# Token order scattered in step t = 9 of the GLU and the ids loaded in step t = 11, instead of t = 10 and t = 12

## The chip, the core and the metric

The kernel runs on one core of a Trainium2 chip. The metric is the device time of one execution in microseconds; smaller is better. One execution was also recorded by the hardware profiler, and every time inside the kernel that is named below is taken from that one recording, counted from the start of its span.

The engines are named as in the profile: PE (matmuls), DVE (the vector engine), ACT (the scalar engine), POOL (GpSimd) and SP (the engine that only issues transfers here).

## The reference

Three stages follow each other: attention with a sliding window and four sink positions, a routed layer with eight experts that gives every token to one expert, and a gated layer over all 1536 tokens.

```python
attn_out = softmax(mask(q @ k.T / 8)) @ v            # 2 x 8 heads x 768 x 64
x = attn_out, heads joined                           # 1536 x 512
e = argmax(x @ w_gate)                               # expert of each token, at most 384 tokens each
y[i] = gate[i] * relu(x[i] @ w1[e]) @ w2[e]          # 0 for a token beyond the 384
out = (sigmoid(y @ w_gate2) * (y @ w_val)) @ w_out   # d_ff = 1536, out is 1536 x 512
```

The last line is the gated layer, called the GLU below.

## The kernel before

**Order of the tokens.** The expert stage leaves the tokens sorted by expert, so row r of the GLU's input is some token of the original order. Which one, `order_ids` and `load_ids` establish: the tile `pi` (one DVE addition, line 701) says for each original token which sorted row it went to; twelve indirect transfers issued by POOL (line 703, one for 128 tokens, four bytes a token) scatter the token numbers into a table `idsd` in DRAM; one transfer issued by SP (line 709) reads the table back as the tile `ids`. The output rows are then written to DRAM with indirect transfers that take their row numbers from `ids`.

```python
def order_ids():
    nc.vector.tensor_tensor(out=pi, in0=pi_a, in1=pi_d, op=ALU.add)
    for i in range(NTILE):
        nc.gpsimd.indirect_dma_start(
            out=idsd_v[i], out_offset=bass.IndirectOffsetOnAxis(ap=pi[:, i:i + 1], axis=0),
...
def load_ids():
    nc.sync.dma_start(out=ids, in_=idsd.rearrange("(j p) o -> p (j o)", p=P))
```

The inputs of `pi`, `pi_a` and `pi_d`, are ready since the expert stage (function `order`, at 150 us).

**The GLU's steps.** The function `glu` works on three chunks of 512 tokens. Each chunk has 12 steps, one for each 128 of the 1536 hidden columns; t counts the steps of all chunks from 0, so t = 9 is the tenth step and t = 12 the first step of the second chunk. Step t does, in this order in the program:

- up to three halves of weight blocks are unpacked in the staging tiles (`conv_a`, lines 153 to 160, ACT and DVE);
- `up`: 24 matmuls (lines 171 to 173) into two banks `g`, then the sigmoid on ACT (line 1023), the product on DVE (1024), and its split into a high part `gh` (ACT, 1025) and a low part `gl` (DVE, 1027);
- at two fixed steps, `order_ids` and `load_ids`;
- the unpacked halves are split into `pair` (`conv_b`, lines 167 and 168), and SP is told to load the next weight block (line 145);
- `down` of the step before: 12 matmuls, three for each of the four banks `acc` (tokens m = 0 to 3 of 128 each);
- if t is the first step of a chunk, `finish` for the chunk that has just ended: for m = 0 to 3 a copy of the bank `acc` into a tile `o` (ACT for m = 0 and 2, line 1075; DVE for m = 1 and 3, line 1073), and `put_out`, the indirect write of that tile by POOL (line 1056).

The tiles `o` come from a pool of three (`cp`, bufs=3). The fourth copy of a chunk, m = 3 on DVE, reuses the tile of m = 0 and so waits until the write of m = 0 has landed. The next matmul into the bank of m = 3 waits for that copy.

**What sets the order.** Each engine runs its instructions in the order in which the program was written, and waits on semaphores for the others. The twelve scatters and the writes of the output stand on POOL's queue, the load of `ids` and the weight loads on SP's. A transfer from POOL signals on one of eight lanes in turn, so the ninth scatter waits until the first has landed.

Of the kernel before, what the change touches and what calls it, by code (L numbers as in the profile page):

```python
# [26 lines left out]
def kernel(  # L27
# [116 lines left out]
    def load_glu(g, q):  # L144
        nc.sync.dma_start(out=stage[q].bitcast(I32), in_=wd[g].bitcast(I32))

    def conv_a(parts, step):

        for q, n0, n1 in parts:
            raw = stage[q].bitcast(I32).rearrange("p (n t) -> p n t", t=2)  # L150
            l_, h_ = raw[:, n0:n1, 0], raw[:, n0:n1, 1]
            if step == 0:
                nc.scalar.activation(out=h_.bitcast(F32), in_=h_.bitcast(F32), func=AF.Copy, scale=2.0 ** -112)
                nc.vector.tensor_scalar(out=l_, in0=l_, scalar1=29, scalar2=None, op0=ALU.logical_shift_right)
            elif step == 1:
                nc.vector.scalar_tensor_tensor(
                    out=l_, in0=h_, scalar=3, in1=l_, op0=ALU.logical_shift_left, op1=ALU.bitwise_or
                )
            else:
                nc.vector.scalar_tensor_tensor(  # L160
                    out=l_, in0=h_, scalar=-2 ** 31, in1=l_, op0=ALU.bitwise_and, op1=ALU.bitwise_or
                )

    def conv_b(q, s, n0, n1, eng):
        f = stage[q].rearrange("p (n t) -> p n t", t=2)[:, n0:n1, 0]
        h_ = slot[s][:, 0, n0:n1]
        nc.scalar.copy(out=h_, in_=f)
        eng.tensor_sub(out=slot[s][:, 1, n0:n1], in0=f, in1=h_.bitcast(F32))
# [531 lines left out]
# [5 lines that stand above are left out]
                in_=ids0[:, i:i + 1], in_offset=None, bounds_check=N - 1, oob_is_err=False,  # L705
            )

    def load_ids():
        nc.sync.dma_start(out=ids, in_=idsd.rearrange("(j p) o -> p (j o)", p=P))
# [261 lines left out]
    def glu(yh, yl):  # L971
        with ExitStack() as st:
# [36 lines left out]
            def up(n, r, w):  # L1009
                ch = n // NPAIR  # L1010
                c = slice(r * P, (r + 1) * P)
                cols = slice(ch * 512, ch * 512 + w)
                pss = []
                for j in range(2):
                    wh, wl = block(n, j)
                    ps = ps_g.tile([P, 512], F32, tag=f"g{j}", name=f"g{j}")[:, :w]
                    for k in range(KD):
                        mm3(ps, wh[:, k, c], wl[:, k, c], yh[:, k, cols], yl[:, k, cols], k == 0, k == KD - 1)
                    pss.append(ps)
                gh = gp.tile([P, 512], F32R, tag="gh", name="gh", bufs=3)  # L1020
                gl = gp.tile([P, 512], F32R, tag="gl", name="gl", bufs=3)
                g = gp.tile([P, 512], F32, tag="g", name="g")[:, :w]
                nc.scalar.activation(out=g, in_=pss[0], func=AF.Sigmoid)  # L1023
                nc.vector.tensor_tensor(out=g, in0=g, in1=pss[1], op=ALU.mult)  # L1024
                nc.scalar.copy(out=gh[:, :w], in_=g)  # L1025
                k = last_rows(w)
                nc.vector.tensor_sub(out=gl[:, :w - k], in0=g[:, :w - k], in1=gh[:, :w - k].bitcast(F32))
                if k:
                    nc.vector.tensor_sub(
                        out=gh[:, w:w + k], in0=g[:, w - k:], in1=gh[:, w - k:w].bitcast(F32)  # L1030
                    )
                return gh, gl
# [5 lines left out]
            def down(t, m, gh, gl, w):  # L1038
                n, r = steps[t]
                wh, wl = block(n, 2)  # L1040
                first, last = t % NF == 0, t % NF == NF - 1
                c = slice(m * P, min(m * P + P, w))
                k = last_rows(w)
                if k and c.stop == w:
                    both = accs[m][:2 * k], gh[:, w - k:w + k], wh[:, r]
                    upper_ = accs[m][:k], gh[:, w - k:w], wl[:, r]
                    if first:
                        nc.tensor.matmul(*both, start=True, stop=False)
                    nc.tensor.matmul(*upper_, start=False, stop=False)
                    if not first:  # L1050
                        nc.tensor.matmul(*both, start=False, stop=last)
                else:
                    mm3(accs[m][:c.stop - c.start], gh[:, c], gl[:, c], wh[:, r], wl[:, r], first, last)

            def put_out(j, o):
                nc.gpsimd.indirect_dma_start(  # L1056
                    out=out_v[j], out_offset=bass.IndirectOffsetOnAxis(ap=ids[:, j:j + 1], axis=0),
                    in_=o, in_offset=None, bounds_check=N - 1, oob_is_err=False,
                )

            def finish(ch, m, w, both=False):
                n = min(P, w - m * P)
                o = zero if n < P else cp.tile([P, 512], F32, tag="o", name="o")
                k = last_rows(w)
                if k and n < P:
                    lo = cp.tile([P, 512], F32, tag="o", name="lo")
                    nc.scalar.copy(out=lo[:k], in_=accs[m][k:2 * k])
                    nc.vector.tensor_tensor(out=o[:k], in0=accs[m][:k], in1=lo[:k], op=ALU.add)
                elif both:
                    nc.scalar.copy(out=o[:n, :256], in_=accs[m][:n, :256])  # L1070
                    nc.vector.tensor_copy(out=o[:n, 256:], in_=accs[m][:n, 256:])
                elif m % 2:
                    nc.vector.tensor_copy(out=o[:n], in_=accs[m][:n])  # L1073
                else:
                    nc.scalar.copy(out=o[:n], in_=accs[m][:n])
                put_out(ch * 4 + m, o)
# [4 lines left out]
            def run(t0, t1, w, half, before):  # L1081

                ch = t0 // NF
                held = []

                for m in range((w + P - 1) // P, 4):
                    put_out(ch * 4 + m, zero)
                for t in range(t0, t1):
                    pend = []
                    n, r = steps[t]  # L1090
                    while half and len(pend) < 3:
                        x, h = half[0]
                        if todo[x][0] > n + 2:
                            break
                        half.pop(0)
                        pend.append((x, h))
                    parts = [(x % 4, h * 512, h * 512 + 512) for x, h in pend]
                    for step in range(3):
                        conv_a(parts, step)
                    g = up(n, r, w)  # L1100

                    if t == 10:
                        order_ids()
                    elif t == 12:
                        load_ids()
                    for x, h in pend:
                        conv_b(x % 4, todo[x][2], h * 512, h * 512 + 512, nc.vector)
                        if h and x + 4 < len(todo):
                            load_glu(todo[x + 4][1], x % 4)
                    if before and t < len(steps) - 2:  # L1110
                        full = w if t > t0 else 512
                        for m in range((full + P - 1) // P):
                            down(t - 1, m, *before, full)
                        if t % NF == 0:
                            for m in range(4):
                                finish(t // NF - 1, m, full)
                    held = (held + [g])[-3:]
                    before = g
                if t1 == len(steps):

                    ms = list(range((w + P - 1) // P))
                    if w % P:
                        ms = ms[-1:] + ms[:-1]
                    for m in ms:
                        down(t1 - 3, m, *held[0], w)
                    for m in ms:
                        down(t1 - 2, m, *held[1], w)
                        down(t1 - 1, m, *held[2], w)
                        finish(ch, m, w, m == ms[-1])
                return before  # L1130
# [117 lines left out]
```

## Time and profile before

| | |
|---|---|
| median of 3 runs | 625.35 us (622.54 to 626.94) |
| the profiled execution, its own time | 624.89 us |
| span of the profiled execution | 623.2 us |
| mean granted PE clock over the span | 0.986 of full |
| PE busy | 599.0 us, 96% of the span |
| DVE busy | 361.0 us, 58% |
| ACT busy | 302.4 us, 49% |
| POOL busy | 107.1 us, 17% |

The span lies 1.7 us under the time of its own execution, and that time 0.5 us under the median. In the rows below a line number L1073 is a line of the kernel, a square bracket in a timeline says how long the engine had been idle before and what ended that, and an x and a number is a count of instructions.

### The profile page before, as it was taken

Reading aid. Unit: us, or ns where it says so; the run is one execution under the profiler, and the core shown is the slowest. Engines: PE = TensorE matmul, PEld = TensorE weight load, DVE = VectorE, ACT = ScalarE, POOL = GpSimd, SP = SyncE. Lnnn points to the kernel's source line nnn. Section 1 sums busy time; section 2 is a strip of 40 time slices with the busy share of each in tenths; the row PEclk is TensorE's granted clock in tenths of the full one; section 3 lists DMA queues with packets and bytes.
Section 4 is the critical chain, followed back from the end, with each engine's and each line's share of the span. In section 5 each row is a group of like instructions: output and inputs, shape, how many; then the busy total and the mean of one; then the engine's idle time right before and its main releaser. Section 6 shows DMA issues by size and latency. Waiting matters only on the chain. (4 is left out here: it accounts for less than half of the span.)

```text
span 623.2 us, 9350 instructions
## 1 busy us (share of the span) xinstructions
PE 599.0 (96%) x3326; PEld 499.4 (80%) x3326; DVE 361.0 (58%) x879; ACT 302.4 (49%) x586; POOL 107.1 (17%) x161
## 2 busy tenths in 40 slices
PE   8999999999999999998999999999699999999995
PEld 4898988957877887886878888888588888999893
DVE  2556466545248838667779999931148811249811
ACT  3578677612268848667556555522025411225411
POOL 3159758360000000000000000034200000200002
PEclk9899999999999999999999999999799999999998
DMA  8989957124029919648335555540203420103001
GB/s 187 304 255 308 341 146 239 55 101 157 0 76 323 347 59 327 260 171 292 115 135 204 199 178 174 191 137 0 69 0 113 170 123 0 68 1 136 1 0 72
DMA packets 43630, 93.97 MB, mean 151 GB/s; under 512 B 5664, under 2 KB 24352, under 8 KB 39728
## 3 DMA queue, kind: packets, MB, share of 16 engines
q1 hardware_dynamic: 39872, 86.24, 41.9%
q0 software_dynamic: 2304, 6.09, 2.6%
q10 hardware_dynamic: 1392, 0.86, 0.5%
q8 instruction: 34, 0.56, 0.4%
q14 instruction: 28, 0.23, 0.1%
HBM read 82.63 MB, written 10.75 MB: 150 GB/s over the span
## 5 line engine op out<-in xcount | busy, mean ns | idle before, releaser
L172 PE MATMUL g<-yl,pair 128*128 128x512 f32 (+1 forms) x288 | 109.0, 379 | 0.3 <-DVE yl L806 0.3
L171 PE MATMUL g<-yh,pair 128*128 128x512 f32 (+1 forms) x288 | 109.1, 379 | 0.2 <-ACT yh L805 0.2
L173 PE MATMUL g<-yh,pair 128*128 128x512 f32 (+1 forms) x288 | 108.8, 378 | 0.0
L1025 ACT CAST gh<-g 128x512 fp32r<-128x512 f32 (+1 forms) x36 | 21.4, 594 | 119.3 <-DVE g L1024 115.3
L1024 DVE TENSOR_TENSOR g<-g,g 128x512 f32<-128x512 f32 (+1 forms) x36 | 23.4, 651 | 83.1 <-PE g L173 68.3
L136 DVE TENSOR_TENSOR pair<-stage,pair 128x1024 fp32r<-128x1024 f32 x54 | 64.5, 1221 | 10.0 <-ACT pair L135 9.8
L135 ACT CAST pair<-stage 128x1024 fp32r<-128x1024 f32 x64 | 65.7, 1051 | 0.8 <-PE u L773 0.8
L773 PE MATMUL u<-pair,hh 128*128 128x512 f32 x224 | 61.7, 401 | 2.8 <-ACT pair L135 1.5
L171 PEld LDWEIGHTS g<-yh,pair 128*128 128x128 f32 x288 | 54.5, 189 | 9.4 <-ACT yh L805 0.7
L172 PEld LDWEIGHTS g<-yl,pair 128*128 128x128 f32 x288 | 54.5, 189 | 8.7 <-issue 0.6
L173 PEld LDWEIGHTS g<-yh,pair 128*128 128x128 f32 x288 | 54.5, 189 | 7.8
L773 PE MATMUL u<-pair,xh 128*128 128x512 f32 x224 | 60.5, 397 | 0.1
L703 POOL DMA_INDIRECT idsd<-ids,pi x12 | 11.8, 983 | 276.5 <-DVE pi L701 273.1
L303 ACT ACTIVATE pt<-sc,neg 128x260 f32<-128x260 f32 (+1 forms) x96 | 44.6, 491 | 26.4 <-DVE neg L292 26.3
L171 PE MATMUL acc<-pair,gh 128*128 128x512 f32 x132 | 51.8, 393 | 5.5 <-DVE o L1073 5.5
L173 PE MATMUL acc<-pair,gl 128*128 128x512 f32 x132 | 51.7, 392 | 0.0
L172 PE MATMUL acc<-pair,gh 128*128 128x512 f32 x132 | 51.7, 392 | 0.0
L773 PEld LDWEIGHTS u<-pair,hh 128*128 128x128 f32 x224 | 40.5, 188 | 13.2 <-issue 4.4
L1023 ACT ACTIVATE g<-g 128x512 f32<-128x512 f32 (+1 forms) x36 | 20.5, 569 | 59.8 <-PE g L173 54.0
L773 PEld LDWEIGHTS u<-pair,xh 128*128 128x128 f32 x224 | 40.8, 188 | 10.2 <-ACT xh L747 1.7
L338 PE MATMUL pv<-v,pts 128*128 128x73 f32 x352 | 43.1, 275 | 0.0
L338 PEld LDWEIGHTS pv<-v,pts 128*128 128x128 f32 x352 | 42.3, 196 | 0.0
(163 smaller groups left out, 1020.3 us busy)
## 6 DMA issues: line engine op xcount, KB each, us to landing
stage<-in_we_dram SPq DMA_DIRECT2D x64, 512.0 KB
stage<-in_wd_dram SPq DMA_DIRECT2D x30, 1024.0 KB
vraw<-in_vr_dram SPq DMA_DIRECT2D x11, 288.0 KB
kraw<-in_kd_dram SPq DMA_DIRECT2D x22, 132.0 KB
qraw<-in_qd_dram SPq DMA_DIRECT2D x22, 128.0 KB
vt<-in_vt_dram SPq DMA_DIRECT2D x11, 256.0 KB
slots<-zero SPq DMA_DIRECT2D x1, 2048.0 KB
xs<-slots SPq DMA_DIRECT2D x8, 256.0 KB
```

What stands on the lines that cost most here:

```text
L135: nc.scalar.copy(out=t[:, 0], in_=raw)
L136: eng.tensor_sub(out=t[:, 1], in0=raw, in1=t[:, 0].bitcast(F32))
L171: nc.tensor.matmul(ps, ah, bh, start=start, stop=False)
L172: nc.tensor.matmul(ps, ah, bl, start=False, stop=False)
L173: nc.tensor.matmul(ps, al, bh, start=False, stop=stop)
L303: nc.scalar.activation(out=pt_[i][:, h, :w], in_=scs_[n][j][:, :w], func=AF.Exp, scale=-1.0, bias=neg_[i][:, h:h + 1],)
L338: nc.tensor.matmul(pv_[n][:, h], pts_[n, h // 2][:, h % 2, j], vb[kb][:, 4 * a + h], start=(h == 0 and j == 0), stop=(h == 3 and j == len( ...
L703: nc.gpsimd.indirect_dma_start(out=idsd_v[i], out_offset=bass.IndirectOffsetOnAxis(ap=pi[:, i:i + 1], axis=0), in_=ids0[:, i:i + 1], in_of ...
L773: nc.tensor.matmul(ps, a, b, start=start, stop=stop)
L1023: nc.scalar.activation(out=g, in_=pss[0], func=AF.Sigmoid)
L1024: nc.vector.tensor_tensor(out=g, in0=g, in1=pss[1], op=ALU.mult)
L1025: nc.scalar.copy(out=gh[:, :w], in_=g)
```

## The change

Two constants change. `order_ids` is called in step t = 9 and not 10, `load_ids` in step 11 and not 12; each stands at the same place within its step.

```diff
                     g = up(n, r, w)
 
-                    if t == 10:
+                    if t == 9:
                         order_ids()
-                    elif t == 12:
+                    elif t == 11:
                         load_ids()
                     for x, h in pend:
                         conv_b(x % 4, todo[x][2], h * 512, h * 512 + 512, nc.vector)
```

On DVE, the place is between the `up` of step 9 and the `up` of step 10. In the names below `g_` and a number is a bank of an `up`, and L168 is the last split of a weight half before the pause in the weight work.

```order
 L1027 TENSOR_TENSOR gl<-g,gh 128x512
+L701 TENSOR_TENSOR pi<-pi_a,pi_d 128x12
 L168 TENSOR_TENSOR pair_91<-stage_84,pair_91 128x512
-L1024 TENSOR_TENSOR g<-g,g_5869 128x512
-L1027 TENSOR_TENSOR gl<-g,gh 128x512
-L701 TENSOR_TENSOR pi<-pi_a,pi_d 128x12
+L1024 TENSOR_TENSOR g<-g,g_5906 128x512
+L1027 TENSOR_TENSOR gl<-g,gh 128x512
```

The addition `pi` moves up over one product, one `gl` and one split; the bank numbers change with the numbering alone.

On SP, the rows around the load of `ids`, with the semaphores that each waits for, are these before:

```order
244 L145 DMA stage_83<-in_wd_dram 128x2048 [waits DMAHW2_49,DVE_49]
245 L145 DMA stage_84<-in_wd_dram 128x2048 [waits DMAHW3_49,DVE_49]
246 L709 DMA ids<-idsd 128x12x1 [waits DMASW4_49,DMASW5_49,DMASW3_49,DMASW6_49,DMASW2_49,DMASW7_49,DMASW1_49,DMASW0_49]
247 L145 DMA stage_85<-in_wd_dram 128x2048 [waits DMAHW4_49,DVE_49]
248 L145 DMA stage_86<-in_wd_dram 128x2048 [waits DMAHW5_49,DVE_49]
```

In the changed kernel these rows are the same, as is all of SP's queue and all of POOL's: no weight load stands between the old place and the new one. The load of `ids` waits for all eight lanes of POOL's transfers (DMASW0 to DMASW7).

## Rows read from the trace of the kernel before

**Rows 1.** The page, part 1: busy time, share of the span and instructions.

```profile
PE 599.0 (96%) x3326; PEld 499.4 (80%) x3326; DVE 361.0 (58%) x879; ACT 302.4 (49%) x586; POOL 107.1 (17%) x161
```

**Rows 2.** The page, part 2: granted PE clock in 40 slices of 15.6 us.

```profile
PEclk9899999999999999999999999999799999999998
```

**Rows 3.** Waits, 430 to 450 us: in total, times, longest.

```profile
DVE o L1073 <- DMA out_dram<-o,ids: 8.9, 1, 8.9
...
PE acc L171 <- DVE o L1073: 5.5, 1, 5.5
```

**Rows 4.** Timeline of PE, 429 to 444 us: start, duration, engine, line.

```profile
430.43 0.39 PE L171 MATMUL g<-yh,pair 128*128 128x512 f32 x1
...
437.69 0.39 PE L173 MATMUL acc<-pair,gl 128*128 128x512 f32 x1
443.52 0.80 PE L171 MATMUL acc<-pair,gh 128*128 128x512 f32 x1 [5.45 <-DVE o L1073]
```

**Rows 5.** Timeline of DVE, 380 to 480 us.

```profile
408.23 0.69 DVE L1027 TENSOR_TENSOR gl<-g,gh 128x512 fp32r<-128x512 f32 x1 [0.69 <-ACT gh L1025]
408.84 0.69 DVE L168 TENSOR_TENSOR pair<-stage,pair 128x512 fp32r<-128x512 f32 x1
411.66 0.69 DVE L1024 TENSOR_TENSOR g<-g,g 128x512 f32<-128x512 f32 x1 [2.13 <-PE g L173]
...
413.65 0.17 DVE L701 TENSOR_TENSOR pi<-pi_a,pi_d 128x12 int32<-128x12 f32 x1
419.82 0.69 DVE L1024 TENSOR_TENSOR g<-g,g 128x512 f32<-128x512 f32 x1 [6.01 <-PE g L173]
...
442.78 0.69 DVE L1073 COPY o<-acc 128x512 f32<-128x512 f32 x1 [8.87 <-DMA out_dram<-o,ids]
```

**Rows 6.** Timeline of POOL, 360 to 623 us.

```profile
414.09 1.02 POOL L703 DMA_INDIRECT idsd<-ids,pi  x1 [273.14 <-DVE pi L701]
...
419.27 0.98 POOL L703 DMA_INDIRECT idsd<-ids,pi  x1 [0.30 <-issue]
...
428.26 0.98 POOL L703 DMA_INDIRECT idsd<-ids,pi  x1 [0.30 <-issue]
439.92 0.98 POOL L1056 DMA_INDIRECT out_dram<-o,ids  x1 [10.68 <-issue]
...
534.84 0.98 POOL L1056 DMA_INDIRECT out_dram<-o,ids  x1 [90.08 <-ACT o L1075]
```

**Rows 7.** Line 709: duration in ns, first and last start in us.

```profile
L709 SPq EVENT_SEMAPHORE  x4: 17/28/28, 432.3 to 435.9; - x4
L709 SPq DMA_DIRECT2D ids<-idsd x1: 377/377/377, 436.0 to 436.0; - x1
```

**Rows 8.** Windows: length, busy time of each engine (count), PE clock, DMA share, GB/s.

```profile
281.40:283.20 1.80, 0.51 (x3) 0.26 (x3) 1.80 (x2) 1.50 (x2) 0.00 (x0) 1.00 0.97 303
...
413.00:415.00 2.00, 2.00 (x10) 1.67 (x9) 0.77 (x2) 0.01 (x1) 0.91 (x1) 1.00 0.30 119
...
441.00:443.00 2.00, 0.00 (x0) 0.00 (x0) 0.22 (x1) 0.00 (x0) 1.49 (x2) 0.60 0.48 184
...
443.52:448.32 4.80, 4.80 (x11) 3.84 (x12) 1.24 (x2) 0.62 (x1) 0.98 (x1) 0.51 0.29 109
...
449.00:451.00 2.00, 2.00 (x10) 1.63 (x9) 0.00 (x0) 0.60 (x1) 0.00 (x0) 1.00 0.03 8
```

**Rows 9.** Timeline of DVE, 525 to 545 us: the next chunk's end.

```profile
539.12 0.69 DVE L1073 COPY o<-acc 128x512 f32<-128x512 f32 x1 [3.75 <-DMA out_dram<-o,ids]
```

**Rows 10.** Waits of PE, 450 to 623 us.

```profile
PE acc L1051 <- DVE gh L1029: 0.3, 1, 0.3
```

**Rows 11.** SP: its timeline, 405 to 445 us.

```profile
409.56 0.33 SPq L145 DMA_DIRECT2D stage<-in_wd_dram  x1
435.95 0.38 SPq L709 DMA_DIRECT2D ids<-idsd  x1
```

**Rows 12.** Waits of SP's queue over the span.

```profile
SPq L145 <- DVE pair L168: 209.1, 18, 65.5
```

**Rows 13.** Line 477, the scatters of the attention stage: min, median and max in ns.

```profile
L477 POOL DMA_INDIRECT slots<-xg,si x12: 977/1083/1223, 38.3 to 131.7; - x12
```

## The prediction

> **What bounds the kernel now.** The page's first part is read first: PE is busy 96% of the span [rows 1], so only work taken off PE, or a hole in PE's row, can move the time much. The second part shows where a hole could be: the granted PE clock is full from the third slice on, with one digit 7 in slice 29, about 436 to 452 us [rows 2]. The waits of that stretch name it: PE waits 5.5 us for the DVE copy L1073, and that copy waits 8.9 us for the first output write to land [rows 3]. This is the first step of the GLU's second chunk, t = 12: the fourth copy of the finished chunk needs the tile of the first, whose write cannot start before `ids` is there.
>
> How much stands in that hole? At full clock 33 matmuls start between 430.43 and 437.69 us, 32 steps in 7.26 us or 0.227 us each, so the next was due at 437.92; it started at 443.52 [rows 4]. That is 5.60 us. Then the clock: it is at 0.60 on average between 441 and 443, so it fell to the lower level (1.2 of 2.4 GHz) in there, after PE had stood still for about 3.3 us, and from 443.52 to 448.32 it was 0.51 while 11 matmuls took 4.80 us; by 449 it was full again [rows 8]. Eleven at 0.227 take 2.50 us, so the slow matmuls lost 2.30. The whole hole is worth 7.90 us, and no change of this chain can give more.
>
> **The chain that ends in the hole.** Link by link: `pi` on DVE starts at 413.65 [rows 5]; the first scatter at 414.09, the twelfth at 428.26, one every 1.29 us, POOL having sat idle 273 us until `pi` [rows 6]; SP's last wait for a scatter ends at 435.9, 7.6 us after the twelfth was issued [rows 7]; the load of `ids` is issued at 435.95 [rows 11]; the first output write follows at 439.92 [rows 6]; the fourth copy starts at 442.78 [rows 5]; PE at 443.52 [rows 4]. From `pi` to the copy that is 29.13 us, and nothing in it but `pi` waits for a step of the GLU. So what counts is how far `pi` moves, not how far `load_ids` does.
>
> **The change part by part.** *`order_ids` one step up.* A step of the GLU at full clock is 36 matmuls, 36 x 0.227 = 8.2 us, but `pi` doesn't move by that. On DVE step 9 was late, behind weight unpacking: its last instruction, L1027, starts at 408.23, and L168 behind it at 408.84 [rows 5]. The new `pi` takes L168's place at 408.84 in place of 413.65: 4.81 us earlier. Its inputs are long there and POOL is idle, so the twelve scatters move by the same 4.81, from 414.09 to 409.28 and from 428.26 to 423.45.
>
> *`load_ids` one step up.* It stands behind the same weight load and ahead of the same one on SP's queue, and POOL's queue is unchanged too. SP comes to it after the load at 409.56 [rows 11] and then waits for the scatters, so the earlier place itself is worth nothing; it only follows the scatters, 435.95 - 4.81 = 431.14. What is queued behind it on SP, the next weight loads, waits for DVE's L168 of later steps, 209.1 us in all over 18 waits [rows 12], so it doesn't come free later than before.
>
> *The rest follows.* Output write at 439.92 - 4.81 = 435.11, fourth copy at 437.97, PE at 438.71, where it was due at 437.92: 0.79 us of the hole is left. Does the clock still fall? A stop of PE of 1.3 us in the window 281.40 to 283.20 left it at 1.00 [rows 8], and the fall in the hole came after some 3.3 us; so no, and the 2.30 us go too. The sum is 4.81 + 2.30 = 7.11 us.
>
> *Costs.* `pi` now stands ahead of L168, which starts 0.17 us later; the DVE instruction behind it idled 2.13 us for PE [rows 5], so this is covered. Were that cover gone, it would cost those 0.17 us. No instruction and no transfer is added.
>
> *What is late next.* After 450 us PE waits 0.3 us in all [rows 10], and the weight loads follow DVE, which follows PE; so all that comes after should slide up by the whole 7.1 us. The end of the next chunk shows the same chain with `ids` already there: its write starts at 534.84 [rows 6], its fourth copy waits 3.75 us until 539.12 [rows 9], and PE doesn't wait at all.
>
> *Bounds of the forecast.* The link that varies is the write's landing: 2.86 us from issue to copy in the first chunk (439.92 to 442.78) but 4.28 in the second (534.84 to 539.12). I take 2.86, since the quiet stretch is the same one; with 4.28, 1.42 us less is gained, 5.7. At the other end the hole closes wholly, 7.9.
>
> *Two rules weighed against it.* The scatters now start while the weight load issued at 409.56 is moving; in the old place they started in the window 413 to 415, where the DMA engines were at 0.30 and after which nothing was loaded [rows 8]. The first scatters may therefore land late, and the ninth waits for the first. Bound: if not one of them moved before 414.09, the chain would be where it is now, and the gain nothing; in between I take half of 4.81. The Trainium skill's page "DMA: Bandwidth & Descriptors", section "Issuing engines are not separate DMA queues", speaks for that: transfers from POOL and from SP run on the same engines and interleave, whoever started them. It is the first rival below.
>
> The other: more DVE work now stands beside the scatters, one L168, one L1024 and one L1027, 0.69 us each. If each held POOL up for its whole length, the chain would lose 2.07 us. Against it speaks the scatter at 419.27, which ran beside the L1024 at 419.82 and took 0.98 us like the others [rows 5, 6]; for it, that in the attention stage, with DVE far busier, a scatter took up to 1.223 us against a least of 0.977 [rows 13]. The Trainium skill's page "SBUF — State Buffer", section "SBUF: two separate sides", has such a rule: a DVE instruction in a mode that uses both ports locks GpSimd out while it writes descriptors. The rows here show no such lock at 419 us.
>
> **The rivals.**
> - *Scatters late beside the weight load.* Gain 2.4 us by the chain instead of 4.81; the hole left is 3.2 us, just short of where the clock fell, so I count the 2.3 us of the clock as half kept: 625.35 - 2.4 - 1.15 = 621.8. For: the overlap is real. Against: a scatter of 128 x 4 bytes is tiny, and only four of the twelve are waited for by others.
> - *DVE holds POOL up.* Gain 4.81 - 2.07 + 2.30 = 5.0, so 620.3. Against: the row at 419.27.
> - *The clock falls all the same.* Gain 4.81 alone: 620.5. Against: the clock stayed up through the other stops after 20 us.
> - *The change doesn't do what it says.* `load_ids` has the same neighbours on SP, so if the scatters did not start from `pi` alone, nothing would move: 625.4. Against: POOL's 273 us of idle ended by `pi` [rows 6].
> - *Slower, by the lane.* Scatter nine, now due at 419.60 us, waits until scatter one has landed. The old ninth was due at 424.4 and went out on time. If the weight load held the first scatter back beyond 424.4, 15 us after its issue, every further microsecond would push the whole chain and PE with it; landing 18 us after its issue it would give about 628. Nothing in the rows is that late: the twelfth took 7.6 us.
>
> **How the numbers follow.** The profiled execution: span 623.2 - 7.1 = 616.1, its own time 624.89 - 7.1 = 617.8. The median of the runs lies 0.46 above that execution, so the forecast is 625.35 - 7.1 = 618.2. Chances: the forecast with its bounds (617.4 to 619.7) 0.68; scatters late 0.14; the clock falls all the same 0.06; nothing moves 0.05; DVE holds POOL up 0.04; slower 0.03. The runs of before spread from 622.54 to 626.94, 0.4% to either side, so a measurement tells about 1%, here 6.3 us, from no change. The forecast lies just beyond that line and its own bounds on both sides of it: I count 0.56 of its 0.68 as faster by over 1%, and the rest, with most rivals, as within 1%; a little of the rivals that keep the clock goes to faster. Of the slower rival only the far end, a landing over 21 us after the issue, would pass 1%. That gives 0.57, 0.41 and 0.02. The range runs from 616.4, the hole closed and a fast draw of the runs, to 621.7, which takes in the clock and the DVE rivals and half of the late scatters.
>
> **What would show it.** In the changed profile: `pi` at 408.8, first scatter near 409.3, one every 1.29 us, last one near 423.5; load of `ids` near 431.1; first output write near 435.1; fourth copy near 438.0; PE's wait for it under 1 us, up to 2.2; no digit under 9 in the clock of slice 29; the rest of the GLU 7 us earlier, with PE still not waiting. Wrong it would be if the scatters' landing stretched (load of `ids` later than 433), if the wait moved to another tile, or if the clock fell somewhere else.

## The result, and the profile after

The changed kernel takes 619.37 us (median of 16 runs, 616.48 to 621.67) against 624.63 (16 runs, 620.84 to 628.61), so the medians are 5.3 us apart. The ratio worked out from all these runs is 0.9904, with a 95% interval from 0.9885 to 0.9924, or 6.0 us less (4.7 to 7.2). The forecast was 7.1 us less and 618.2 us, with a range of 616.4 to 621.7. The profiled execution has a span of 617.9 us.

The runs of one kernel spread by up to 0.6% either way, and the profile shows part of why. This is the granted clock of the changed kernel in 40 slices, to be read beside [rows 2]:

```profile
PEclk9999999999999999997999999999999999999998
```

The 7 of slice 29 is gone, but a 7 stands in slice 19, in the expert stage, where the kernel before had none. That stage isn't touched by the change, and the two spans differ for this reason too. So the change is read in the stage that it touches: from the first matmul of line 172, where the GLU begins, to the issue of the last output write. Before, that is 327.18 to 617.43 us, 290.25 us; after, 327.90 to 612.54, 284.64 us. The GLU is 5.61 us shorter, and this is the number to explain.

The waits of the changed kernel, 400 to 450 us, answer to [rows 3]:

```profile
DVE o L1073 <- DMA out_dram<-o,ids: 8.8, 1, 8.8
...
PE acc L171 <- DVE o L1073: 2.1, 1, 2.1
```

PE still waits for the fourth copy, but 2.1 us in place of 5.5. Its timeline, as in [rows 4]:

```profile
438.37 0.39 PE L173 MATMUL acc<-pair,gl 128*128 128x512 f32 x1
440.85 0.50 PE L171 MATMUL acc<-pair,gh 128*128 128x512 f32 x1 [2.09 <-DVE o L1073]
```

The next matmul was due at 438.37 + 0.23 = 438.60, so the hole is 2.25 us in place of 5.60. The clock stayed at 1.00 in every window of 2 us from 436 to 460, so the 2.30 us of slow matmuls are gone. These are the two windows around the hole, as in [rows 8]:

```profile
438.00:440.00 2.00, 0.76 (x4) 0.30 (x2) 0.00 (x0) 0.00 (x0) 1.39 (x3) 1.00 0.34 131
440.00:442.00 2.00, 1.15 (x5) 0.97 (x6) 1.28 (x2) 0.57 (x1) 1.70 (x2) 1.00 0.67 256
```

Both together are 5.65 us (5.60 - 2.25 + 2.30), against the 5.61 measured. DVE, POOL and the load of `ids` on SP, as in [rows 5, 6, 11]:

```profile
408.90 0.69 DVE L1027 TENSOR_TENSOR gl<-g,gh 128x512 fp32r<-128x512 f32 x1 [0.69 <-ACT gh L1025]
409.51 0.16 DVE L701 TENSOR_TENSOR pi<-pi_a,pi_d 128x12 int32<-128x12 f32 x1
409.60 0.68 DVE L168 TENSOR_TENSOR pair<-stage,pair 128x512 fp32r<-128x512 f32 x1
...
440.11 0.69 DVE L1073 COPY o<-acc 128x512 f32<-128x512 f32 x1 [8.77 <-DMA out_dram<-o,ids]
```

```profile
409.95 1.22 POOL L703 DMA_INDIRECT idsd<-ids,pi  x1 [272.23 <-DVE pi L701]
411.48 0.98 POOL L703 DMA_INDIRECT idsd<-ids,pi  x1 [0.30 <-issue]
412.76 0.98 POOL L703 DMA_INDIRECT idsd<-ids,pi  x1 [0.30 <-issue]
414.04 1.22 POOL L703 DMA_INDIRECT idsd<-ids,pi  x1 [0.30 <-issue]
...
421.48 0.97 POOL L703 DMA_INDIRECT idsd<-ids,pi  x1 [1.09 <-issue]
...
425.33 0.98 POOL L703 DMA_INDIRECT idsd<-ids,pi  x1 [0.30 <-issue]
437.26 0.98 POOL L1056 DMA_INDIRECT out_dram<-o,ids  x1 [10.95 <-issue]
```

```profile
433.21 0.38 SPq L709 DMA_DIRECT2D ids<-idsd  x1
```

All of this execution lies 0.67 us later by step 9 (L1027 at 408.90 against 408.23), and in that frame `pi` moved by exactly the 4.81 us forecast. But from `pi` to the fourth copy it is now 440.11 - 409.51 = 30.60 us, not 29.13. Of the 1.47 more, 1.21 lie between the first and the twelfth scatter (15.38 us against 14.17): two scatters took 1.22 us, the first and the fourth, where they had taken 1.02 and 0.98, and the ninth began 1.09 us after the end of the eighth and not 0.30, which is 0.79 more. The other 0.26 lie behind the twelfth scatter. For the ninth's delay the profile names nothing that POOL waited for (`<-issue`).

### The profile page after: what moved, and what is told of

The parts are those of the page before. It is cut to its first block, busy times and chain, and to the rows that moved or that the text cites. A ratio compares the mean times of both kernels' runs of the same rounds, so it can differ in the third digit from the quotient of the medians.

```text
span 617.9 us, 9350 instructions
## 1 busy us (share of the span) xinstructions
PE 596.4 (97%) x3326; PEld 496.9 (80%) x3326; DVE 361.6 (59%) x879; ACT 302.5 (49%) x586; POOL 107.4 (17%) x161
## 5 line engine op out<-in xcount | busy, mean ns | idle before, releaser
L1024 DVE TENSOR_TENSOR g<-g,g 128x512 f32<-128x512 f32 (+1 forms) x36 | 23.4, 649 | 77.6 <-PE g L173 66.0
```

## The experiments

No run takes one of the two constants alone. By the order of the queues it would show nothing new: with `order_ids` in 9 and `load_ids` left in 12 every queue holds the same instructions in the same order as the changed kernel, and with 10 and 11 the same as the kernel before. That the move of `load_ids` is worth nothing is argued from this order, as in the prediction.

The table puts all runs side by side. GLU is the stretch defined above, and hole is the time that PE stood still behind the fourth copy. (The copy belongs to step 12; the matmul that waits for it is in the `down` of step 13.) Chain is `pi` to the fourth copy. The clock column says whether the granted clock fell in the hole or within 2 us behind it. The stretches are read from one recorded execution of each kernel; the ratio is to runs of the kernel before that were taken along with it, with its 95% interval.

| run | GLU, us | hole, us | clock | chain, us | ratio to before |
|---|---|---|---|---|---|
| before | 290.25 | 5.60 | fell | 29.13 | 1 |
| changed | 284.64 | 2.25 | full | 30.60 | 0.9904 (0.9885 to 0.9924) |
| e1, scatter in t = 8 | 286.42 | 2.44 | fell | 36.38 | 0.9944 (0.9918 to 0.9970) |
| e2, before, tile of its own | 282.28 | 0 | full | | 0.9883 (0.9849 to 0.9916) |
| e3, before, PE kept busy | 288.89 | 1.70 idle | full | 30.04 | 0.9949 (0.9925 to 0.9973) |
| e4, load behind the ids | 286.05 | 3.63 | full | 31.95 | 0.9956 (0.9923 to 0.9989) |
| e5, scatter in t = 11 | 298.78 | 14.28 | fell | 29.65 | 1.0147 (1.0089 to 1.0205) |
| e6, load in t = 13 | 284.47 | 2.05 | full | 30.39 | 0.9880 (0.9839 to 0.9921) |
| e7, scatter in t = 4 | 295.83 | 0 | fell earlier | | 1.0042 (1.0008 to 1.0077) |
| e8, changed, tile of its own | 282.27 | 0 | full | | 0.9831 (0.9789 to 0.9872) |
| e9, pi behind the split | 286.21 | 2.16 | fell | 29.89 | one execution |
| e10, changed again | 284.79 | 2.34 | full | 30.67 | one execution |

**e2: the fourth copy gets a tile of its own.** The places of before are kept.

```diff
                 o = zero if n < P else cp.tile([P, 512], F32, tag="o", name="o")
+                if ch == 0 and m == 3:
+                    o = gp.tile([P, 512], F32, tag="gl", name="o4", bufs=3)
```

> The kernel before with its old places, but the fourth copy of the first chunk goes to a tile of its own (a free buffer of the gl tiles), so that it needn't wait for the first output write. Theory (the tile reuse is what ties PE to the ids): the copy runs at once, hole 0 though the ids come as late as before, clock full, gain 7.9 us, ratio 0.987. Rival (PE would meet the late ids elsewhere, at a later tile or bank): a new wait of several us within the next steps, ratio 0.995 or above.

The two copies on DVE in its timeline (m = 1 and 3; the line is 1075 in this kernel, which has two lines more), and the only wait of PE from 430 us on:

```profile
438.82 1.28 DVE L1075 COPY o<-acc 128x512 f32<-128x512 f32 x2
```

```profile
PE acc L1051 <- DVE gh L1029: 0.3, 1, 0.3
```

Both copies run back to back, and PE doesn't wait for the fourth copy, although the first output write is issued as late as 445.93. The GLU is 7.97 us shorter than before, against 7.90 forecast for the whole hole; the ratio 0.9883 agrees with 0.987. No new wait takes the hole's place. This shows the reuse of the tile to be what ties PE to the ids, and prices the hole with its clock.

**e8: the same tile in the changed kernel.**

> The changed kernel and the tile of its own for the fourth copy together. Theory (the change acts through the fourth copy's wait alone): hole 0, and the same time as with that tile and the old places, ratio 0.987 to 0.989. Rival (the change is worth something besides, or costs something, by the scatters beside the last weight load): a ratio off that by over 0.3%.

The GLU takes 282.27 us against 282.28 in e2: with the wait for the tile gone, the change is worth nothing in the GLU, and costs nothing. The ratio of 0.9831 lies off e2's 0.9883 by more than the 0.3% that the rival named, but the two intervals overlap, and the traces show no difference in the GLU. These two are the fastest versions, at medians of 615.31 and 616.69 us.

**e5: the scatter one step later.** From the kernel before:

```diff
-                    if t == 10:
+                    if t == 11:
                         order_ids()
```

> The kernel before with the scatter one step later (order_ids in t = 11, load_ids left in t = 12). Theory (in the stretch without weight loads the chain from pi to the fourth copy has a fixed length near 29 us, so each us of pi is a us of the hole): pi 8.2 us later, hole 13.7 us in place of 5.6, chain 28.5 to 30 us, clock lost about as before; ratio 1.013. Rival (something else than pi holds the ids, and pi's place counts only in part): hole under 10 us, ratio under 1.008.

```profile
423.21 0.16 DVE L701 TENSOR_TENSOR pi<-pi_a,pi_d 128x12 int32<-128x12 f32 x1
...
452.86 0.69 DVE L1073 COPY o<-acc 128x512 f32<-128x512 f32 x1 [20.80 <-DMA out_dram<-o,ids]
```

Counted from the start of the GLU, `pi` is 8.16 us later than before, and the chain is 29.65 us, 0.52 longer. The hole grows by the sum of both, 8.68 us, and the GLU by 8.53. So in the stretch without weight loads each microsecond of `pi` is a microsecond of the hole.

**e3: PE kept busy with matmuls of no use.** From the kernel before:

```diff
+                            if t == NF and m == 3:
+                                idle = ps_g.tile([P, 512], F32, tag="g0", name="idle")
+                                for _ in range(22):
+                                    nc.tensor.matmul(idle, ones, ones.unsqueeze(1).to_broadcast([P, 4, P]), start=True, stop=True)
                             down(t - 1, m, *before, full)
```

> The kernel before with 22 extra matmuls of no use in the hole at t = 12, just ahead of the matmuls that wait for the fourth copy. Theory (of the 7.9 us, 2.3 are the clock that falls while PE stands still): the granted clock stays at 1.00 through 441 to 448, the wait for the copy ends where it did, gain 2.3 us, ratio 0.996. Rival (the fall costs nothing, since the matmuls after it have slack, or it comes all the same): ratio 1.000.

The edit doesn't put the matmuls quite where the expectation has them. They run ahead of the last three matmuls of the finished chunk, a step before the hole, and so make all of PE's later work 5 us late instead of filling the hole itself:

```profile
433.14 4.92 PE L1116 MATMUL idle<-ones 128*128 128x512 bf16 x22
...
447.82 0.50 PE L171 MATMUL acc<-pair,gh 128*128 128x512 f32 x1 [1.55 <-DVE o L1073]
```

For the question it comes to the same: PE stands still for 1.70 us and not for the 5.60 of before, and the clock is 1.00 in all windows from 438 to 450. The GLU is 1.36 us shorter, in an execution whose chain was 0.91 longer (30.04 against 29.13), and 2.30 - 0.91 = 1.39. So the clock's 2.30 us of the hole are shown apart from the idle time; the ratio's interval holds the 0.996.

**e1: the scatter one more step up.** From the changed kernel:

```diff
-                    if t == 9:
+                    if t == 8:
                         order_ids()
```

> The scatter one more step up (order_ids in t = 8, load_ids in t = 11). Theory (the hole in PE at t = 12 goes with the place of pi on DVE, link by link): pi starts 5.6 us earlier than in the changed kernel, so even with a chain 1.5 to 4 us longer than the 29.1 us of before the fourth copy is ready before PE wants the bank; hole 0, clock full, gain about 7.9 us, ratio to before 0.987. Rival (the scatters lose to the weight loads that they now run beside what they gain by the earlier start): the ninth scatter waits several us for the first, the hole stays at 2 us or more, ratio 0.990 or above.

```profile
404.46 1.19 POOL L703 DMA_INDIRECT idsd<-ids,pi  x1 [0.31 <-issue]
...
414.14 0.98 POOL L703 DMA_INDIRECT idsd<-ids,pi  x1 [0.30 <-issue]
421.45 0.98 POOL L703 DMA_INDIRECT idsd<-ids,pi  x1 [6.32 <-DMA idsd<-ids,pi]
```

The rival won. The tenth scatter waited 6.32 us for an earlier one to land. With eight lanes taken in turn that is the second, which had been issued at 404.46 and so had not landed until just before 421.45, 17 us later. Two weight loads were issued around that time, at 403.88 and 408.93. Counted from the start of the GLU, `pi` came 5.6 us earlier than in the changed kernel, the chain is 5.8 us longer, and the hole is about as large as in the changed kernel (2.44 us against 2.25).

**e7: the scatter in t = 4.** The same line of the changed kernel, with 4.

> The scatter in t = 4 (load_ids in t = 11): more than 40 us ahead of the need, among five weight loads. Theory (the scatters and the weight loads slow each other, but with this lead the ids are still in time): the chain may take over 36 us, hole 0, clock full; the weight loads land some us later than before, which their own lead covers; ratio 0.987. Rival (late weight loads stop PE, through the unpacking on ACT and DVE): new waits of PE in the steps 4 to 9, ratio 0.99 or above.

The rival won again, and this time the kernel is slower than before. Waits, 360 to 425 us:

```profile
ACT stage L153 <- DMA stage<-in_wd_dram: 13.2, 4, 5.6
...
PE acc L171 <- ACT gh L1025: 8.7, 3, 5.4
POOL idsd L703 <- DMA idsd<-ids,pi: 7.6, 1, 7.6
```

The hole behind the fourth copy is closed, but the weight loads now come late: ACT waits 13.2 us for them, and PE 8.7 us behind ACT, while the clock falls to 0.50 between 410 and 416. The kernel before has no such wait of ACT or PE in this stretch. The scatters are slow as well: by the profile's table of transfers the twelve took 14.6 us at the median from issue to landing, against 7.7 in e6. So the slowing is mutual.

**e4 and e6: no weight load beside the scatters.** In the changed kernel, the load of step 9 is issued by SP behind the ids load (e4), or by ACT in step 13 (e6):

```diff
                         if h and x + 4 < len(todo):
-                            load_glu(todo[x + 4][1], x % 4)
+                            if t == 9:
+                                late.append((todo[x + 4][1], x % 4))
+                            else:
+                                load_glu(todo[x + 4][1], x % 4)
...
+                    for g_, q_ in late if t == 13 else []:     # e6
+                        nc.scalar.dma_start(out=stage[q_].bitcast(I32), in_=wd[g_].bitcast(I32))
...
                         load_ids()
+                        for g_ in late:                        # e4
+                            load_glu(*g_)
```

> The changed kernel with the weight load of step t = 9 issued behind the load of the ids, so that no weight load runs beside the scatters from 410 us on. Theory (1.5 us of the forecast were lost because the scatters ran beside that load): the ninth scatter goes out on time, pi to fourth copy is back at 29.1 to 29.7 us in place of 30.6, the hole shrinks from 2.2 to about 1 us, ratio about 0.988. Rival (the scatters are held up by DVE or land late by themselves): the chain stays at 30.6 us and the hole at 2.2.

> The changed kernel with the weight load of step t = 9 issued by ACT in step t = 13, behind the fourth copy, so that it meets neither the scatters nor the load of the ids. Theory (the weight load beside the scatters costs the ninth scatter its 0.8 us, and nothing else of the chain): the ninth goes out 1.3 to 1.5 us after the eighth, the ids load is back at 4.0 us from issue to first output write, the chain is 29.6 to 30.2 us in place of 30.6, the hole 1.2 to 1.8 us, no fall of the clock; ratio 0.989. Rival (the weight load is not what holds the scatters): chain 30.6 us and ninth scatter late again. The first scatter, which starts under a split on DVE, still takes 1.22 us by either.

In both the ninth scatter goes out on time, 0.30 us behind the end of the eighth; in the changed kernel it was 1.09. But the chain hardly gains by that: in both, the tenth scatter then took 1.45 us, and the link from the ids load to the first write, 3.97 us before and 4.05 after, took 4.6 us in e6 and 5.5 in e4. For e6 that isn't the edit's doing, since this link took 4.4 to 4.8 us in e1 to e3, e5 and e8 to e10 too. In e4 SP issued the weight load right behind the ids load:

```profile
435.25 0.38 SPq L709 DMA_DIRECT2D ids<-idsd  x1
435.72 0.66 SPq L145 DMA_DIRECT2D stage<-in_wd_dram  x1
```

So e4 probably traded one overlap for another; no run holds this apart from the spread of the link. The expectations for e4 and e6 were holes of about 1 us and of 1.2 to 1.8; they were 3.63 and 2.05. The weight load is at most a part of the 1.47 us.

**e9 and e10: which scatters are slow.** In e9 `order_ids` is called behind the splits of step 9, so that `pi` follows L168; e10 is the changed kernel once more.

```diff
-                    if t == 9:
-                        order_ids()
...
                         if h and x + 4 < len(todo):
                             load_glu(todo[x + 4][1], x % 4)
+                    if t == 9:
+                        order_ids()
```

> The changed kernel with pi behind the split L168 of step t = 9 and not ahead of it. Theory (a scatter that begins while a DVE instruction with two SBUF inputs is running waits for it, 0.2 to 0.5 us): pi starts 0.6 us later, but the first scatter is clear of L168 and the fourth of L1027, so both take 0.98 us in place of 1.22; one of the later ones may meet the L1027 of step 11 and take 1.2 to 1.45. Rival (the first and the fourth scatter are slow by themselves): they take 1.22 again.

> The changed kernel once more, one look. Theory (the ninth scatter's 0.8 us of waiting in the changed kernel's profile is a matter of that execution, and the holds by DVE are not): the first and the fourth scatter take 1.22 us again, the ninth goes out on time and the tenth then meets the L1027 and takes 1.45; pi to ids load 22.7 to 23.5 us, hole 1.5 to 2.5 us. Rival (the weight load holds the ninth each time): the ninth waits 0.8 us again.

POOL in e10, then in e9:

```profile
410.60 1.22 POOL L703 DMA_INDIRECT idsd<-ids,pi  x1 [270.41 <-DVE pi L701]
...
414.69 1.20 POOL L703 DMA_INDIRECT idsd<-ids,pi  x1 [0.30 <-issue]
...
421.42 0.98 POOL L703 DMA_INDIRECT idsd<-ids,pi  x1 [0.40 <-DMA idsd<-ids,pi]
422.70 1.35 POOL L703 DMA_INDIRECT idsd<-ids,pi  x1 [0.30 <-issue]
```

```profile
408.34 1.02 POOL L703 DMA_INDIRECT idsd<-ids,pi  x1 [268.77 <-DVE pi L701]
...
412.23 0.98 POOL L703 DMA_INDIRECT idsd<-ids,pi  x1 [0.30 <-issue]
...
419.94 1.26 POOL L703 DMA_INDIRECT idsd<-ids,pi  x1 [0.30 <-issue]
```

In e9 the first and the fourth scatter are back at 1.02 and 0.98, and the tenth, which begins 0.28 us into the L1027 at 419.66, takes 1.26. In e10 the first and the fourth are slow again, the ninth waits 0.1 us more than usual, and the tenth, which begins in an L1027, takes 1.35. So the holds by DVE come with the place each time. The ninth's delay doesn't: it was 0.79 us in the changed kernel's profile, 0.10 in e10 and none in e8 and e9, all four with the weight load in its place. What made it 0.79 in that one execution stays open.

## Why the prediction was right, and where it was off

**The hole and its price: right.** 5.60 us of idle time and 2.30 of clock stood there, 7.90 in all: e2 gives back 7.97, e3 shows the clock's part alone, and all that comes after slides with PE. In the runs whose clock stayed full (changed, e4, e6, e10) the GLU is within 0.2 us of 282.27 plus the hole; in those where it fell the rest, the clock's part, is 2.4 us (before, counted as 2.30 from its matmuls), 2.2 (e5), 1.7 (e1) and 1.8 (e9).

**What moves: right.** `pi` moved by the 4.81 us forecast, and the chain hangs on `pi` (e5). SP's load of `ids` followed the scatters.

**The length of the chain: the term that was mis-sized.** The prediction moved 29.13 us as a whole and left 0.79 us of the hole, 2.2 at the far bound. The chain measured 30.60 us and left 2.25; so the gain was 5.65 us by the trace and not 7.11, and the ratio came to lie just inside the 1% line that the forecast had put it just outside of. That the far bound was met so closely is luck. It stood for a later landing of the output write, and this link was 2.85 us, the 2.86 of before. The 1.47 us arose elsewhere, in three parts:

- Some 0.4 us are shown: scatters that begin under certain DVE instructions of steps 9 to 11 take 0.2 to 0.5 us longer each, 0.48 us against the usual 0.98 in the changed kernel (two of 1.22) and 0.8 to 1.0 in e4, e6, e8 and e10 (three). The prediction had this as a rival and gave it 4%, resting on a scatter that ran beside an L1024. It asked the wrong row, as the last section tells.
- 0.79 us are the ninth scatter's delay, whose cause is open.
- 0.26 us lie behind the twelfth scatter, within the spread of these links. In e3 and e5, with `pi` in the quiet stretch, the chain was 30.04 and 29.65 us, so the 29.13 of the recording was at the short end. In e5 the excess lies between the ids load and the first write (4.60 us against 3.97); in e3 half of it lies there (4.40), and half between the twelfth scatter and the ids load. Where it comes from isn't settled.

In e10, the same kernel once more, the chain is 30.67 us, but of other parts: three slow scatters, 0.10 us for the ninth, and 4.74 us from the ids load to the first write. That the two agree so well is chance.

**Scatters beside the weight load: the mechanism is real, its size here small.** This rival had 14%. Its first half came true: until the weight load was nearly through, none of the scatters' packets moved. These are the transfer queues of the changed kernel, with packets, MB and share of the time, from 409.9 to 414.3 us and then from 414.3 to 416 (the other queues of the second stretch are left out). POOL's transfers are on q0, SP's weight load is on q1, and four scatters were issued in the first stretch:

```profile
q1 hardware_dynamic: 127, 1.04, 69.5%
```

```profile
q0 software_dynamic: 125, 0.00, 5.3%
```

The prediction's bound says that if no scatter moved before 414.09, the gain would be nothing. Here none moved before 414.3, which is 413.6 in the time of the kernel before, and yet the gain was 5.65 us. The step doesn't hold because POOL went on issuing meanwhile: only the ninth scatter needs the first to have landed, and it went out 11.5 us after the first. One load beside the first scatters cost 0 (e8, e9) to at most 0.8 us. With `pi` one step further up the wait for a lane was 6.3 us (e1), and in t = 4 both sides lose (e7). The "slower by the lane" rival said that a first scatter landing over 15 us after its issue would push the whole chain; in e1 the second landed 17 us after its issue and did so, but `pi` was early enough there for the kernel to stay faster than before.

**The clock: right for the recorded executions, for a reason that doesn't hold.** The prediction took the 3.3 us before the fall in the old hole as a measure of what a stop must last. In e1 and e9 the clock fell with holes of 2.44 and 2.16 us; in the changed kernel, e6, e10 and e4 it stayed up with 2.25, 2.05, 2.34 and 3.63. So a hole of the size that is left can cost the clock, 1.7 and 1.8 us in e1 and e9. That the clock's 2.30 us came in is in part luck. Both recorded executions of the changed kernel kept the clock; in how many of the others it fell isn't known.

## What to carry to other kernels

When a wait is at the end of a long chain, find the one link that waits for the loop and ask how far that link moves; the step number in the source is not the answer, and a call further down the same queue with nothing between is none. Then ask whether the chain must end in the loop at all: one more buffer at its end (e2) was worth more than the earlier start, and doesn't depend on how long the chain takes. An earlier start isn't free: small scatters among large loads came late, and in e7 the loads did too. Of the steps tried, 4 and 8 to 11, the best was 9, the last one in which a weight load is issued, and not the earliest.

## What the runs showed of the hardware that was not expected

**DVE holds a scatter, but not every DVE instruction does.** Scatters that began while an L168, L160 or L1027 (both inputs in SBUF) had 0.3 us or more to go took 1.20 to 1.50 us in place of 0.98, with one exception in e7, where an L168 had begun 0.02 us before the scatter. The excess follows what the DVE instruction still had to run: 0.24 us for 0.32 to go (e10, first scatter), 0.28 for 0.40 (e9, tenth), 0.47 for 0.60 (e6, tenth). Scatters that began under an L1024, whose one input is a PSUM bank, took 0.98, with up to 0.65 us of it to go. A DVE instruction that began during a scatter changed neither: the scatter took 0.98 and the L1027 its usual 0.69. The Trainium skill's page "SBUF — State Buffer", section "Who interferes with whom", has such a rule: a DVE instruction with two SBUF inputs contends with a GpSimd instruction that reads SBUF, and the second to start waits. The rows agree with it where the scatter is the second; no row shows a DVE instruction held by a scatter that began before it. Where that section of the Trainium skill reports that a `tensor_tensor` was not seen to stall a DMA, the rows differ: L168 and L1027 are both TENSOR_TENSOR. Nor does the rule cover L154, which has one input, and under which scatters took 1.19 us (e1, e7) and 1.23 (e7).

**The length of a stop of PE doesn't fix whether its clock falls.** Granted clock in windows of 2 us: e9, with a hole of 2.16 us, then e4, with 3.63. In e9 PE was back at 438.54, and the clock fell only after that.

```profile
438.00:440.00 2.00, 1.46 (x6) 1.24 (x7) 1.31 (x3) 0.62 (x1) 1.47 (x2) 1.00 0.56 213
440.00:442.00 2.00, 2.00 (x6) 1.58 (x5) 0.46 (x1) 0.00 (x0) 0.00 (x0) 0.51 0.34 131
442.00:444.00 2.00, 2.00 (x7) 1.52 (x7) 0.00 (x0) 0.07 (x1) 0.00 (x0) 0.64 0.00 0
```

```profile
442.00:444.00 2.00, 0.00 (x0) 0.00 (x0) 0.29 (x1) 0.00 (x0) 1.68 (x2) 1.00 0.58 221
444.00:446.00 2.00, 1.54 (x7) 1.28 (x8) 1.31 (x3) 0.62 (x1) 1.27 (x2) 1.00 0.45 172
446.00:448.00 2.00, 2.00 (x10) 1.64 (x9) 0.38 (x1) 0.00 (x0) 0.00 (x0) 1.00 0.34 131
```

**Scatters of four bytes land slowly even with no load beside them.** In all runs with `pi` in steps 8 to 11, 7.2 to 8.2 us pass from the issue of the twelfth scatter to the issue of the ids load that waits for it, whereas the copy that waits for the first output write, of 2 KB rows, starts 2.9 us after that write's issue (3.0 in e4).
